# Attention scores head by head in quarters of the TensorE array, and the turned probabilities copied in two parts

## The chip, the cores and the metric

The kernel runs on one core of one Trainium2 chip. The time is that of the whole program on the device in microseconds (us); three runs of the kernel before took 480.45, 480.79 and 478.44 us, median 480.45 us.

TensorE multiplies, VectorE (DVE), ScalarE (ACT) and GpSimd (POOL) work on tiles of 128 partitions, and SyncE (SP) issues most DMAs. In the profile a product on TensorE is two instructions: PEld loads its stationary operand (its weights), PE streams the moving operand through them. A product of fp32 operands shows as two such pairs.

## What is computed

Attention over keys and values averaged in groups of 8, then a mixture of experts on the rows of its output. The shapes: batch 8, heads 8, sequence 576, head size 64, so 4608 tokens of 512 numbers; 8 experts with 1024 hidden units.

```python
k_p = k.reshape(B, H, Sp, pool, D).mean(axis=3)        # Sp = 72 pooled keys
v_p = v.reshape(B, H, Sp, pool, D).mean(axis=3)
scores = scale * np.matmul(q, k_p.transpose(0, 1, 3, 2))
scores = scores - np.max(scores, axis=-1, keepdims=True)
attn = np.exp(scores)
attn = attn / (np.sum(attn, axis=-1, keepdims=True) + 1e-09)
x = np.matmul(attn, v_p)                               # rows of tokens, 512 wide
...
do_compute = x @ w_skip > 0
e_idx = np.argmax(x @ w_gate, axis=1)                  # one expert per token
h = np.maximum(x[mask] @ w1[e], 0.0)
out = x + gate_w * (h @ w2[e])                         # where do_compute
```

## The kernel before

**Stages.** The first stage, attention, takes the 4608 tokens in 36 tiles of 128 queries (in the program t = 0 to 35). A tile belongs to one batch or, for t = 4, 13, 22 and 31, half to one and half to the next. While it runs, the routing of finished tiles to experts is worked out in seven groups (9, 5, 4, 6, 5, 4 and 3 tiles), GpSimd scatters the token numbers of each tile into a table in DRAM (L415), and the weights of one chosen expert are staged and split in high and low parts. The second stage runs the experts, from about 147 us on; first with products for three tiles gathered early (L532 to L552), then in a loop over units of tokens.

**A step of the attention stage.** All engines' orders are fixed when the program is written (a manual schedule; no scheduler moves anything). In step t of the loop at L842 the order is:

1. ScalarE copies the turned probabilities of tile t-2 from PSUM to SBUF, `turned_p` (L328: one instruction, 640 columns); in steps that begin a new batch also the turned sums of values, `turned_v` (L267).
2. VectorE normalises tile t-3 (L355 to L362), whose output rows SyncE stores (L361).
3. TensorE makes the scores of tile t (`scores`, L303). Heads lie two and two on the partitions (head size 64 twice). The 8 heads are 4 pairs; the pooled keys of a pair stand in `kbd` as a block diagonal, so one product of 128 x 128 queries with 144 columns makes both heads of a pair. Pairs 0 and 1 go to one PSUM bank, pairs 2 and 3 to another. A tile on two batches does each product in two halves of 64 queries.
4. VectorE takes minima (L309, one instruction a bank), and ScalarE the exponentials, 8 of 128 x 72 (L315), into `e`.
5. TensorE multiplies the probabilities of tile t-2 with the values (`values`, L341 and L344, 12 pairs of weights and product), then turns the probabilities of tile t-1 (`turn_p`, L323 and L324, five transposes into two PSUM banks `pt`); in some steps it then turns sums of values (`turn_v`, L261 and L262).
6. VectorE, ScalarE and GpSimd do what is due of the side work: sums of keys (L208), key blocks (L213), splitting of weights (L582, L585, L589), steps of the routing (L380 to L465), scatters (L415).

`pt` exists once, the values' bank `o` (L335) once, the probabilities `e` and their copy `pT` twice, the scores' banks three times for two a tile. So the copy of step t waits for the transposes at the end of step t-1, the values wait for the copy and for the normalising of tile t-3, and the transposes come after the values.

**Start and end.** Tiles 0 and 1 are scored before the loop; pair g can be scored as soon as its keys are summed (L208) and laid out (L213). At the end VectorE turns the counts into slots, and when the last scatter has landed GpSimd fetches rows of the table (L1040), TensorE turns them (L1072), and VectorE takes them as slots (L1073 to L1075). On TensorE L1072 stands between the early products in a fixed place; a barrier of all engines follows before the loop over units.

The three lines that fix the places of scores:

```python
sc = ps_s.tile([128, 512], F32, name="sc")[:, 0:4 * SP]          # L300, one bank of half the heads
nc.tensor.matmul(sc[sl, g * 2 * SP:(g + 1) * 2 * SP], qts[t // QG][:, t % QG, half * 2 + g, sl],
                 kbd[b % 2][:, half * 2 + g, :], start=True, stop=True)   # L303
```

Of the kernel before, what the change touches and what calls it, by code (L numbers as in the profile page):

```python
# [26 lines left out]
F32 = mybir.dt.float32  # L27
# [18 lines left out]
VA = HD + 10  # L46
# [117 lines left out]
def attention(tc, nc, q, k, vm, vr, cf, wg, w1, w2, whi, wlo, out, c, pay, offs, table, near, bufs, late, early, mb, fin, cfs):  # L164
    with ExitStack() as ctx:
# [92 lines left out]
        def turn_v(b):  # L258
            tp = pt[:, 1, 128:512].rearrange("p (j n) -> p j n", j=3)
# [39 lines left out]
        def scores(t, half):  # L299
            sc = ps_s.tile([128, 512], F32, name="sc")[:, 0:4 * SP]  # L300
            for g in range(2):
                for sl, b in parts(t):
                    nc.tensor.matmul(sc[sl, g * 2 * SP:(g + 1) * 2 * SP], qts[t // QG][:, t % QG, half * 2 + g, sl],  # L303
                                     kbd[b % 2][:, half * 2 + g, :], start=True, stop=True)
            return sc
# [5 lines left out]
        def exped(e, sc, mn, i):  # L311
            ev = e[:, (4 * SP + GAP) * i:(4 * SP + GAP) * i + 4 * SP].rearrange("p (k g) -> p g k", g=2)
            for h in range(4):
                k0 = (h % 2 ^ i) * SP
                nc.scalar.activation(ev[:, h // 2, k0:k0 + SP], sc[:, h * SP:(h + 1) * SP], AF.Exp,  # L315
                                     bias=mn[:, 4 * i + h:4 * i + h + 1], scale=-1.0)

        def turn_p(e):
            for i in range(2):
                k0 = (4 * SP + GAP + 2 * KL) * i  # L320
                ev = e[:, k0:k0 + 256].rearrange("p (k g) -> p g k", g=2)
                for g in range(2):
                    nc.tensor.transpose(ptf[:, (2 * i + g) * 128:(2 * i + g) * 128 + 128], ev[:, g], ident)  # L323
            nc.tensor.transpose(ptf[:, 512:640], e[:, 256:384], ident)  # L324

        def turned_p():
            pT = ap.tile([128, 5, 128], F32, name="pT")
            nc.scalar.activation(flat(pT), ptf[:, 0:640], AF.Copy)  # L328
            return pT

        def values(t, pT, apart=False):
# [5 lines left out]
            for a, o_ in enumerate(os):  # L337
                ov = o_[:, 0:4 * VA].rearrange("p (g h c) -> p g h c", g=2, h=2)
                for g in range(2):
                    for sl, b in parts(t):  # L340
                        nc.tensor.matmul(o_[sl, g * 2 * VA:(g + 1) * 2 * VA], pT[:, 2 * a + g, sl], vbd[b % 2][:, 2 * a + g, :],  # L341
                                         start=(g == 0), stop=False)
                for sl, b in parts(t):
                    nc.tensor.matmul(ov[sl, :, 1, :], pT[:, 4, sl], vl4[b % 3][:, 2 * a:2 * a + 2, :], start=False, stop=True)  # L344
# [466 lines left out]
        def exponentials(t, sc, mn):  # L811
            es[t] = ebuf[t % 2]
            for i in range(2):
                exped(es[t], sc[i], mn, i)
# [4 lines left out]
        for t in range(2):  # L819
# [3 lines left out]
            sc = [scores(t, i) for i in range(2)]  # L823
# [13 lines left out]
        sc = [scores(2, i) for i in range(2)]  # L837
# [4 lines left out]
        for t in range(2, NT):  # L842
# [11 lines left out]
            if t > 2:  # L854
                normal(t - 3)
                sc = [scores(t, i) for i in range(2)]
# [933 lines left out]
```

## Time and profile before

| what | value |
|---|---|
| median of three runs | 480.45 us (478.44 to 480.79) |
| the profiled execution: time, span | 481.24 us, 479.2 us |
| instructions in the span | 11182 |
| PE busy | 463.5 us (97%), x3043 |
| PEld busy | 417.1 us (87%), x3044 |
| DVE, ACT, POOL busy | 303.4 (63%), 225.7 (47%), 250.3 us (52%) |
| granted TensorE clock, mean | 0.999 |
| HBM read, written | 80.85 MB, 31.21 MB |

The span runs from the first to the last instruction; the profiled execution's own time is 2.0 us longer. Busy is the time in which at least one instruction of an engine was under way. Matmuls are pipelined: a product's duration holds the way through the array, and products of a stream overlap, so that the pace of a stream is read from starts, not from durations. Idle time has a releaser, the instruction that ended the wait as far as the profile shows ("issue": none shown).

### The profile page before, as it was taken

The page shows a single profiled execution, that of the slowest core. Times are in us where ns is not written, and L with a number is a line of the kernel's source. Part 1 is how long each engine was busy: PE and PEld are TensorE (multiplying, and loading weights), DVE is VectorE, ACT ScalarE, POOL GpSimd, SP SyncE. Part 2 cuts the span into 40 slices and gives each one's busy share as a digit, 9 for nine tenths or more (in the row PEclk, how much of TensorE's full clock was granted, in tenths as well). Part 3 has the DMA queues.
Part 4 walks back from the last instruction along what each step waited for, and adds up shares of the span by engine and source line. Part 5 has one row for each costly group of instructions (what it writes and reads, how often), then busy time and mean ns, then how long its engine had stood idle before and what let it go on. Part 6 is the DMA issues. An engine that isn't in the chain of part 4 may idle for free. (4 is left out here: it accounts for less than half of the span.)

```text
span 479.2 us, 11182 instructions
## 1 busy us (share of the span) xinstructions
PE 463.5 (97%) x3043; PEld 417.1 (87%) x3044; DVE 303.4 (63%) x713; ACT 225.7 (47%) x578; POOL 250.3 (52%) x328
## 2 busy tenths in 40 slices
PE   7999999999999999899999999999999999999995
PEld 4799899989999979798989987989899898989894
DVE  5877888798788622578795667663846554343321
ACT  5678768888891211546462645612435251212110
POOL 4499499999998154363342424362624161515242
PEclk9999999999999999999999999999999999999999
DMA  8999999996931026679787497877687223322021
GB/s 278 388 396 390 361 352 332 384 333 207 328 122 68 11 62 215 230 228 308 247 289 244 136 290 241 300 240 251 202 256 262 89 95 101 129 66 88 22 88 42
DMA packets 52042, 103.88 MB, mean 217 GB/s; under 512 B 10031, under 2 KB 22959, under 8 KB 50336
## 3 DMA queue, kind: packets, MB, share of 16 engines
q1 hardware_dynamic: 40544, 78.18, 47.8%
q0 software_dynamic: 11456, 25.22, 15.0%
q8 instruction: 17, 0.28, 0.2%
q14 instruction: 25, 0.20, 0.1%
HBM read 80.85 MB, written 31.21 MB: 234 GB/s over the span
## 5 line engine op out<-in xcount | busy, mean ns | idle before, releaser
L1289 POOL DMA_INDIRECT out<-ring,slot x33 | 35.8, 1085 | 109.3 <-POOLq L1115 105.6
L315 ACT ACTIVATE e<-sc,mn 128x72 f32<-128x72 f32 x288 | 65.0, 345 | 7.4 <-DVE mn L309 6.8
L1527 ACT ACTIVATE hhi<-psl 128x256 fp32r<-128x256 f32 (+3 forms) x59 | 23.5, 400 | 94.0 <-ACTq L1115 93.5
L1384 PE MATMUL psl<-xlo,w1hi 128*128 128x256 f32 (+3 forms) x220 | 64.1, 291 | 0.0
L1383 PE MATMUL psl<-xhi,w1hi 128*128 128x256 f32 (+3 forms) x220 | 64.0, 291 | 0.0
L1385 PE MATMUL psl<-xhi,w1lo 128*128 128x256 f32 (+3 forms) x220 | 64.0, 291 | 0.0
L1284 POOL DMA_INDIRECT ring<-out,slot x42 | 46.6, 1109 | 22.6 <-issue 22.4
L341 PE MATMUL o<-vbd,pT 128*128 128x148 f32 (+1 forms) x312 | 49.4, 298 | 1.1 <-DVE x L360 1.1
L1626 DVE SCALAR_TENSOR_TENSOR hlo<-psl,hhi 128x256 fp32r<-128x256 f32 (+2 forms) x55 | 23.2, 423 | 41.3 <-DVEq L1115 39.0
L415 POOL DMA_INDIRECT table<-pay,r_di x36 | 36.7, 1018 | 12.6 <-DVE mb L443 6.4
L1383 PEld LDWEIGHTS psl<-xhi,w1hi 128*128 128x128 f32 x220 | 41.3, 188 | 0.8 <-issue 0.4
L1384 PEld LDWEIGHTS psl<-xlo,w1hi 128*128 128x128 f32 x220 | 41.3, 188 | 0.5
L341 PEld LDWEIGHTS o<-vbd,pT 128*128 128x128 f32 (+1 forms) x312 | 38.6, 179 | 3.6 <-ACT ring L213 1.0
L1385 PEld LDWEIGHTS psl<-xhi,w1lo 128*128 128x128 f32 x220 | 41.2, 187 | 0.0
L1297 POOL DMA_DIRECT2D sorted<-ring x39 | 22.2, 572 | 32.9 <-DMA ring<-out,slot 25.8
L1603 DVE TENSOR_TENSOR w2lo<-stage,w2hi 128x1024 fp32r<-128x1024 f32 x28 | 34.3, 1223 | 6.6 <-DVEq L1115 6.4
L1384 PE MATMUL psd<-xlo,w1hi 128*128 128x256 f32 (+3 forms) x132 | 38.4, 291 | 0.0
L1385 PE MATMUL psd<-xhi,w1lo 128*128 128x256 f32 (+3 forms) x132 | 38.4, 291 | 0.0
L1383 PE MATMUL psd<-xhi,w1hi 128*128 128x256 f32 (+3 forms) x132 | 38.4, 291 | 0.0
L1409 PE MATMUL mb<-w2hi,hlo 128*128 128x512 f32 x88 | 34.8, 396 | 0.0
L1409 PE MATMUL psf<-w2hi,hlo 128*128 128x512 f32 x88 | 34.8, 396 | 0.0
L1407 PE MATMUL psf<-w2hi,hhi 128*128 128x512 f32 x88 | 34.8, 395 | 0.0
(276 smaller groups left out, 1216.0 us busy)
## 6 DMA issues: line engine op xcount, KB each, us to landing
stage<-in_w SPq DMA_DIRECT2D x64, 512.0 KB, 5.5
sorted<-ring POOLq DMA_DIRECT2D x39, 256.0 KB, 3.3
out<-x SPq DMA_DIRECT2D x36, 256.0 KB, 5.4
stage<-in_k SPq DMA_DIRECT2D x6, 1152.0 KB, 8.8
blocks<-sorted SPq DMA_DIRECT2D x100, 64.0 KB
qt<-in_q SPq DMA_DIRECT2D x9, 512.0 KB, 7.4
hhi<-in_vm SPq DMA_DIRECT2D x4, 1024.0 KB, 7.7
hlo<-in_vm SPq DMA_DIRECT2D x3, 1024.0 KB, 9.8
```

Of the source, the lines that this page charges most:

```text
L315: nc.scalar.activation(ev[:, h // 2, k0:k0 + SP], sc[:, h * SP:(h + 1) * SP], AF.Exp, bias=mn[:, 4 * i + h:4 * i + h + 1], scale=-1.0)
L341: nc.tensor.matmul(o_[sl, g * 2 * VA:(g + 1) * 2 * VA], pT[:, 2 * a + g, sl], vbd[b % 2][:, 2 * a + g, :], start=(g == 0), stop=False)
L415: m = nc.gpsimd.indirect_dma_start(table, bass.IndirectOffsetOnAxis(ap=di[:, j:j + 1], axis=0), flat(fin["pays"][:, t0 + j:t0 + j + TW // ...
L1284: g.indirect_dma_start(ring[:, (s + 3) % 9, 0:D], None, out, bass.IndirectOffsetOnAxis(ap=slot[:, s:s + 1], axis=0), bounds_check=NTOK - 1 ...
L1289: g.indirect_dma_start(out, bass.IndirectOffsetOnAxis(ap=offsets, axis=0), ring[:, (s + 3) % 9, 0:D], None, bounds_check=NTOK - 1, oob_is_ ...
L1383: t.matmul(ps, whi[0][:, k, w], xhi[:, k, xs], start=(k == 0), stop=False)
L1384: t.matmul(ps, whi[0][:, k, w], xlo[:, k, xs], start=False, stop=False)
L1385: last = t.matmul(ps, wlo[0][:, k, w], xhi[:, k, xs], start=False, stop=(k == 3))
L1407: t.matmul(ps, hhi[:, k, sl], whi[1][:, k, :], start=(k == 0), stop=False)
L1409: last = t.matmul(ps, hlo[:, k, sl], whi[1][:, k, :], start=False, stop=(k == 7))
L1527: a.activation(hhi[:, f, xs], bank(f, xs, alone), AF.Relu).then_inc(sem["act"], 1)
L1603: v.tensor_tensor(chunk_of(wlo, c), chunk_view(stage[c], c), chunk_of(whi, c).bitcast(F32), ALU.subtract).then_inc(sem["wlo1" if c < 4 els ...
```

## The change

The scores of a tile are made head by head. A head lies on one half of the partitions, so each product takes 64 partitions of queries, 64 queries and the 72 columns of its own keys: 16 products a tile instead of 4 (or 8 in a tile on two batches), each in one quarter of the array (half of its rows, half of its columns). The order is pair by pair; within a pair first the lower 64 queries, then the upper; within these first the head on the lower partitions, then the one on the upper. Heads on the lower partitions go to one PSUM bank, those on the upper to the other; the exponentials follow this order, to the same places of `e`. `kbd` keeps its layout; its zeros are not read any more. The copy of the turned probabilities becomes two instructions of 384 and 256 columns, one from each bank of `pt`, to two tiles; the transposes go three to the first bank and two to the second, and `turn_v` uses other columns of the two banks.

```diff
         def turn_v(b):
-            tp = pt[:, 1, 128:512].rearrange("p (j n) -> p j n", j=3)
+            tp = ptf[:, 384:768].rearrange("p (j n) -> p j n", j=3)
             for j in range(2):
                 nc.tensor.transpose(tp[:, j, :], vss[b][:, j * 128:j * 128 + 128], ident)
             nc.tensor.transpose(tp[:, 2, :], lss[b], ident)
@@ -296,36 +296,41 @@
             b0, b1 = t * 128 // S, (t * 128 + 127) // S
             return [(slice(0, 128), b0)] if b0 == b1 else [(slice(0, 64), b0), (slice(64, 128), b1)]
 
-        def scores(t, half):
-            sc = ps_s.tile([128, 512], F32, name="sc")[:, 0:4 * SP]
-            for g in range(2):
-                for sl, b in parts(t):
-                    nc.tensor.matmul(sc[sl, g * 2 * SP:(g + 1) * 2 * SP], qts[t // QG][:, t % QG, half * 2 + g, sl],
-                                     kbd[b % 2][:, half * 2 + g, :], start=True, stop=True)
+        def scores(t):
+            sc = [ps_s.tile([128, 512], F32, name="sc")[:, 0:4 * SP] for _ in range(2)]
+            for g in range(4):
+                for i, sl in enumerate(halves):
+                    b = (t * 128 + i * 64) // S
+                    for r, o in zip(halves, range(2)):
+                        nc.tensor.matmul(sc[o][sl, g * SP:(g + 1) * SP], qts[t // QG][r, t % QG, g, sl],
+                                         kbd[b % 2][r, g, o * SP:(o + 1) * SP], start=True, stop=True)
             return sc
 
         def least(sc, mn, i):
 
             nc.vector.tensor_reduce(mn[:, i * 4:i * 4 + 4], sc.rearrange("p (h k) -> p h k", k=SP), axis=AX.X, op=ALU.min)
 
-        def exped(e, sc, mn, i):
-            ev = e[:, (4 * SP + GAP) * i:(4 * SP + GAP) * i + 4 * SP].rearrange("p (k g) -> p g k", g=2)
-            for h in range(4):
-                k0 = (h % 2 ^ i) * SP
-                nc.scalar.activation(ev[:, h // 2, k0:k0 + SP], sc[:, h * SP:(h + 1) * SP], AF.Exp,
-                                     bias=mn[:, 4 * i + h:4 * i + h + 1], scale=-1.0)
+        def exped(e, sc, mn, o):
+            for g in range(4):
+                i = g // 2
+                ev = e[:, (4 * SP + GAP) * i:(4 * SP + GAP) * i + 4 * SP].rearrange("p (k g) -> p g k", g=2)
+                k0 = (o ^ i) * SP
+                nc.scalar.activation(ev[:, g % 2, k0:k0 + SP], sc[:, g * SP:(g + 1) * SP], AF.Exp,
+                                     bias=mn[:, 4 * o + g:4 * o + g + 1], scale=-1.0)
 
         def turn_p(e):
             for i in range(2):
                 k0 = (4 * SP + GAP + 2 * KL) * i
                 ev = e[:, k0:k0 + 256].rearrange("p (k g) -> p g k", g=2)
                 for g in range(2):
-                    nc.tensor.transpose(ptf[:, (2 * i + g) * 128:(2 * i + g) * 128 + 128], ev[:, g], ident)
-            nc.tensor.transpose(ptf[:, 512:640], e[:, 256:384], ident)
+                    nc.tensor.transpose(pt[:, i, (2 * i + g) * 128:(2 * i + g) * 128 + 128], ev[:, g], ident)
+                if i == 0:
+                    nc.tensor.transpose(pt[:, 0, 256:384], e[:, 256:384], ident)
 
         def turned_p():
-            pT = ap.tile([128, 5, 128], F32, name="pT")
-            nc.scalar.activation(flat(pT), ptf[:, 0:640], AF.Copy)
+            pT = [ap.tile([128, 3 - i, 128], F32, name=f"pT{i}") for i in range(2)]
+            for i, sl in enumerate((slice(0, 384), slice(256, 512))):
+                nc.scalar.activation(flat(pT[i]), pt[:, i, sl], AF.Copy)
             return pT
 
         def values(t, pT, apart=False):
@@ -338,10 +343,10 @@
                 ov = o_[:, 0:4 * VA].rearrange("p (g h c) -> p g h c", g=2, h=2)
                 for g in range(2):
                     for sl, b in parts(t):
-                        nc.tensor.matmul(o_[sl, g * 2 * VA:(g + 1) * 2 * VA], pT[:, 2 * a + g, sl], vbd[b % 2][:, 2 * a + g, :],
+                        nc.tensor.matmul(o_[sl, g * 2 * VA:(g + 1) * 2 * VA], pT[a][:, g, sl], vbd[b % 2][:, 2 * a + g, :],
                                          start=(g == 0), stop=False)
                 for sl, b in parts(t):
-                    nc.tensor.matmul(ov[sl, :, 1, :], pT[:, 4, sl], vl4[b % 3][:, 2 * a:2 * a + 2, :], start=False, stop=True)
+                    nc.tensor.matmul(ov[sl, :, 1, :], pT[0][:, 2, sl], vl4[b % 3][:, 2 * a:2 * a + 2, :], start=False, stop=True)
             return [o_.unsqueeze(1) for o_ in os] if apart else [o]
 
         def normalised(t, os):
@@ -810,8 +815,8 @@
 
         def exponentials(t, sc, mn):
             es[t] = ebuf[t % 2]
-            for i in range(2):
-                exped(es[t], sc[i], mn, i)
+            for o in range(2):
+                exped(es[t], sc[o], mn, o)
@@ -820,7 +825,7 @@
...
-            sc = [scores(t, i) for i in range(2)]
+            sc = scores(t)
             exponentials(t, sc, softmax(t, sc))
...
```

On TensorE, in a step in which a tile's queries are of one batch (names: `sc` scores, `pT` the copied probabilities, `pt` the PSUM they are turned in), the rows before, from the scores to the transposes:

```order
L303 MATMUL sc<-ring,qt 128x144 [waits DMAHW3_49]
L303 MATMUL sc<-ring,qt 128x144
L303 MATMUL sc<-ring,qt 128x144 [waits DVE_49,Activation_49]
L303 MATMUL sc<-ring,qt 128x144
L341 MATMUL o<-vbd_121,pT 128x148 [waits DVE_49,Activation_49]
L341 MATMUL o<-vbd_121,pT 128x148
L344 MATMUL o<-vl_123,pT 128x2x74
L341 MATMUL o<-vbd_121,pT 128x148 x2
L344 MATMUL o<-vl_123,pT 128x2x74
L323 MATMUL pt<-cfs,e_127 128x128 x4
L324 MATMUL pt<-cfs,e_127 128x128
```

and the same step now:

```order
L305 MATMUL sc<-ring,qt 64x72 [waits DMAHW3_49]
L305 MATMUL sc<-ring,qt 64x72 [waits DVE_49,Activation_49]
L305 MATMUL sc<-ring,qt 64x72 x14
L346 MATMUL o<-vbd_121,pT_685 128x148 [waits DVE_49,Activation_49]
L346 MATMUL o<-vbd_121,pT_685 128x148
L349 MATMUL o<-vl_123,pT_685 128x2x74
L346 MATMUL o<-vbd_121,pT_686 128x148 [waits Activation_49]
L346 MATMUL o<-vbd_121,pT_686 128x148
L349 MATMUL o<-vl_123,pT_685 128x2x74
L326 MATMUL pt<-cfs,e_127 128x128 x2
```

Four products became sixteen in the same place; the wait for ScalarE's exponentials of the tile before moved from the third product to the second, and the second half of the values has a wait of its own for the second copy.

At the start of the program on TensorE, from the first scores to the first transposes of tile 1, before:

```order
L303 MATMUL sc<-ring,qt 128x144 [waits DMAHW1_49,Activation_49,Pool_49]
L303 MATMUL sc<-ring,qt 128x144 [waits Activation_49] x3
L303 MATMUL sc<-ring,qt 128x144 [waits DMAHW5_49]
L303 MATMUL sc<-ring,qt 128x144
L303 MATMUL sc<-ring,qt 128x144 [waits DVE_49,Activation_49]
L303 MATMUL sc<-ring,qt 128x144
L817 MATMUL o<-ring 128x512
```

and now:

```order
L305 MATMUL sc<-ring,qt 64x72 x2
L305 MATMUL sc<-ring,qt 64x72 [waits Activation_49] x2
L305 MATMUL sc<-ring,qt 64x72 x2
L305 MATMUL sc<-ring,qt 64x72 [waits DMAHW5_49]
L305 MATMUL sc<-ring,qt 64x72 [waits DVE_49,Activation_49]
L305 MATMUL sc<-ring,qt 64x72 x14
L822 MATMUL o<-ring 128x512
```

Both banks of tile 0 are now complete only after the keys of the last pair, and all of tile 1 but its first product stands behind the wait for exponentials of tile 0.

## Rows read from the trace of the kernel before

**Rows 1.** Windows by stage: PE, PEld, DVE, ACT, POOL busy (x instructions), PEclk, DMA share, GB/s.
```profile
50.00:75.00 25.00, 24.39 (x214) 22.89 (x214) 22.18 (x81) 19.16 (x69) 17.91 (x19) 1.00 0.97 356
```

**Rows 2.** Timeline of one step, all engines: start us, us, what [idle before <-releaser].
```profile
85.55 0.27 PE L324 MATMUL pt<-cfs,e 128*128 128x128 f32 x1
...
85.66 1.15 PE L303 MATMUL sc<-ring,xhi 128*128 128x144 f32 x8
...
85.92 0.71 ACT L328 ACTIVATE pT<-pt 128x640 f32<-128x640 f32 x1 [0.30 <-PE pt L324]
...
86.68 0.55 PEld L341 LDWEIGHTS o<-vbd,pT 128*128 128x128 f32 x4
...
88.76 0.27 PE L324 MATMUL pt<-cfs,e 128*128 128x128 f32 x1
...
88.89 0.68 DVE L360 TENSOR_TENSOR x<-o,rc 128x512 f32<-128x512 f32 x1
```

**Rows 3.** Timeline of PE and PEld about tiles on two batches, four stretches.
```profile
122.86 0.27 PE L262 MATMUL pt<-cfs,ls 128*128 128x128 f32 x1
123.06 1.20 PE L303 MATMUL sc<-ring,xlo 128*64 128x144 f32 x16
...
123.06 0.14 PEld L303 LDWEIGHTS sc<-ring,xlo 128*64 128x64 f32 x2 [0.17 <-issue]
...
33.81 0.29 PE L344 MATMUL o<-ring,pT 128*64 128x148 f32 x1
...
34.03 0.32 PEld L323 LDWEIGHTS pt<-cfs,e 128*128 128x128 f32 x2 [0.20 <-issue]
```

**Rows 4.** Timeline of PE: short products of the routing.
```profile
91.60 0.26 PE L399 MATMUL mb<-r_oh,ones 128*128 128x40 bf16 x4
...
91.71 0.18 PE L401 MATMUL mb<-r_oh,upper 128*128 128x32 bf16 x1
```

**Rows 5.** Timeline of POOL, first and last scatter; windows of POOL between.
```profile
55.78 1.08 POOL L415 DMA_INDIRECT table<-pay,r_di  x1 [6.39 <-DVE mb L443]
...
58.35 0.99 POOL L415 DMA_INDIRECT table<-pay,r_di  x1 [0.17 <-issue]
...
155.03 0.98 POOL L415 DMA_INDIRECT table<-pay,r_di  x1 [0.30 <-issue]
...
125.00:152.40 27.40, 24.77 (x30) 1.00 0.47 167
```

**Rows 6.** The source line L1072: duration ns min/median/max, first and last start us.
```profile
L1072 PEld LDWEIGHTS o<-cfs,stage x2: 189/190/191, 162.6 to 162.8; 81*128 81x128 f32 x2
...
L1072 PEldq EVENT_SEMAPHORE  x1: 1459/1459/1459, 160.7 to 160.7; - x1
```

**Rows 7.** Timeline of the start: ACT, DVE, PE.
```profile
8.78 0.54 ACT L213 ACTIVATE ring<-kp 64x72 f32<-64x72 f32 x2 [0.25 <-DVE kp L208]
9.34 3.73 ACT L315 ACTIVATE e<-sc,mn 128x72 f32<-128x72 f32 x16
...
8.66 0.45 DVE L309 TENSOR_REDUCE mn<-sc 128x4 f32<-128x288 f32 x1
...
13.71 0.75 PE L323 MATMUL pt<-cfs,e 128*128 128x128 f32 x4 [0.30 <-ACT pT L328]
```

**Rows 8.** Timeline of DVE, the normalising that opens step 11.
```profile
48.56 0.21 DVE L355 RECIPROCAL rc<-o 128x8 f32<-128x8 f32 x1 [0.53 <-PE o L344]
```

**Rows 9.** Timeline of ACT: a copy of 384 columns.
```profile
27.89 0.48 ACT L267 ACTIVATE vT<-pt 128x384 f32<-128x384 f32 x1
```

**Rows 10.** Windows after the last product; then groups of PE by shape, mean ns last.
```profile
474.30:477.90 3.60, 0.00 (x0) 0.00 (x0) 0.75 (x1) 0.00 (x0) 0.97 (x1) 1.00 0.03 10
478.20:479.10 0.90, 0.00 (x0) 0.00 (x0) 0.00 (x0) 0.00 (x0) 0.00 (x0) 0.50 0.20 75
...
L739 PE MATMUL o<-ring 128*128 128x512 f32 x6 | 5.5, 1084 | 1.7 <-POOL ring L717 1.7
...
L817 PE MATMUL o<-ring 128*128 128x512 f32 x6 | 3.1, 593 | 0.0
```

More of the change, by code (lines that the diff above doesn't have):

```diff
@@ L836, in attention @@
         gates_dve(0)
-        sc = [scores(2, i) for i in range(2)]
+        sc = scores(2)
         mn = softmax(2, sc)
@@ L855, in attention @@
                 normal(t - 3)
-                sc = [scores(t, i) for i in range(2)]
+                sc = scores(t)
             if t == NT - 1:
```

## The prediction

> **What bounds the kernel now.** I read a window of the attention stage first. From 50 to 75 us TensorE is busy for 24.39 of 25 us, DVE for 22.18 and ACT for 19.16 [rows 1]. The change touches only the attention stage, so the questions are what ends a step there, and whether a shorter stage makes the rest start earlier.
>
> The timeline of one step answers the first. I measure from T, the start of the last transpose (85.55). ACT starts the copy of the probabilities at T+0.37, it takes 0.71, and the weights of the values are loaded at 86.68, T+1.13. In between TensorE does the scores, from 85.66 on: 8 products in 1.15, their last start 0.29 before the end, so 0.123 each, and the stream is over at T+1.09. The next T is 88.76, 2.08 after the values' load; the step lasts 3.21 [rows 2]. So scores and copy run side by side and end within 0.04 us of each other: shorter scores help only as far as the copy gets shorter too. A third loop is as tight: the normalising of the step's x ends at 88.89 + 0.68 = 89.57, 2.89 after the values' load [rows 2], and the next values must wait for it.
>
> The second answer is GpSimd. It waits 6.39 us for the routing of the first nine tiles, starts the first scatter at 55.78 and the last at 155.03. In between it is never free: the idle times before scatters are 0.17 or 0.30 with no releaser, and from 125 to 152.4 it is busy for 24.77 of 27.4 us with that 0.17 between its instructions [rows 5]. The last scatter leads to the fetched table rows, for which TensorE's queue waited at L1072 from 160.7 for 1.459 us, until 162.16; the weights there were loaded at 162.6 [rows 6]. So TensorE comes to that place only some 0.5 us after the data. **Whatever TensorE gains beyond 0.5 us, it waits off at L1072, unless GpSimd's chain starts earlier at 55.78.**
>
> **The change part by part.**
>
> *Switch to quarters.* A plain step has no switch of the array's shape now; the tiles on two batches have. There the first load of half-width weights comes 0.20 after the start of the last full transpose (122.86 to 123.06), where a load inside a stream is ahead of its product [rows 3]. Back, the next full load comes 0.22 after the start of the last half-width product (33.81 to 34.03); 0.126 of this is its 148 columns, so 0.09 remains [rows 3]. The trace shows no quarter; I take these two for it, since they are the nearest, also half a shape.
>
> *Sixteen products for four.* With half the columns each (72 for 144) a pair of instructions streams for 0.061 instead of 0.123 [rows 2]. Whether quarters run side by side is not shown, but halves are: 16 pairs of 144 columns took 1.20, where 8 full ones took 1.15 [rows 2, 3]. So each half did its own 8 in the full pace. Four quarters side by side: first load 0.05 (what 1.20 has over 7 paces and the last 0.29), 7 paces of 0.061, and some 0.02 of offset: 0.50. Lower bound of the stretch: this. Upper bound: all 32 pairs one after another, 1.95. A middle: what feeds them, since four short products began between 91.60 and 91.71, one each 0.027 [rows 4], 0.86 for 32. I take 0.50, nearest to the rows on halves, which are also fp32 products with their own weights.
>
> The scores then end, and a load may follow, at T + 0.20 + 0.50 + 0.06 + 0.09 = T+0.85, before it was T+1.09.
>
> *Two copies for one.* 384 columns take 0.48 [rows 9], 640 take 0.71 [rows 2], so 256 take some 0.37, together 0.14 more; consecutive copies overlap by about 0.1, which leaves 0.05 on ACT. The second copy has no wait for TensorE in the changed order, so the first waits for all five transposes: it starts at T+0.37 as now and ends at T+0.85; the values follow at T+0.90. The second copy ends some 0.3 later, and its half of the values comes 0.75 later: hidden. **A plain step saves 0.23, of which I take 0.20**, because ACT now gets its minima after both banks and its 8 exponentials end later against T, and because the x of the step is ready at 2.89 + 0.05 after the values' load where TensorE could be there after 2.08 + 0.90 = 2.98, so that any other DVE work eats the rest. In steps that begin a batch the copy of the value sums follows the two copies, and TensorE waits for that; I count 0.05 lost.
>
> *Exponentials, minima, values, place of the turned sums:* same number, same size, same queue; nothing, hidden or not. No DMA is added or moved.
>
> *The start.* Before, half of tile 0's heads are ready with the second pair of keys: the minimum is taken at 8.66 and the exponentials start at 9.34, right after the last keys (8.78 + 0.54) [rows 7]. Now both banks need the last keys: products and their way through the array 0.4, the minimum 0.45, so the exponentials start at about 10.25, 0.9 late. Behind the second product of tile 1 all of its scores wait for tile 0's first four exponentials (to 11.2), are done at 12.0, and the exponentials of tile 1 start at 12.5 instead of going on without a break: they end at 14.3 instead of 13.07. Transposes of tile 1 waited for the first copy until 13.71 [rows 7]; they come at 14.7, 1.0 late. TensorE's next scores give back 0.3: **0.65 lost at the start**, with 0 (if keys of later steps come from DMA no earlier anyway) and 1.2 as bounds.
>
> *Until the first scatter.* The nine tiles' routing hangs on step 11's normalising (48.56) [rows 8]. Steps 4 to 10 come before: five plain ones save 1.0, two that begin a batch lose 0.1. With the start: 1.0 - 0.1 - 0.65 = 0.25 us earlier.
>
> *The sum.* GpSimd's chain, and with it the data for L1072, comes 0.25 earlier; TensorE's own 0.5 of delay there goes. Gain 0.75 us; the profiled execution would take 481.24 - 0.75 = 480.5. It lies 0.8 above the median of the runs, so I predict 480.45 - 0.75 = **479.7 us**. TensorE saves some 3 us more in steps 11 to 35 (about 20 plain ones, some held by DVE), and waits them off at L1072, some 2.5 us.
>
> **The rivals.**
>
> *GpSimd does not hold it.* If its chain gets shorter by as much as the steps, the 3.25 us all count: 477.2. For it: TensorE is the busiest engine [rows 1]. Against it: no idle time between its scatters but the fixed one [rows 5]. Chance 0.15.
>
> *The quarters are fed too slowly* (0.86 for the 32 pairs): scores end at T+1.2, no step saves, the start's loss stays: 481.2. The half-width loads speak against it: two begun within 0.14, each of them that long [rows 3]. Chance 0.08.
>
> *Weight loads on the same rows queue up.* Loads of 64 columns come 16 in 0.93 + 0.14 [rows 3], which alone would also fit loads one behind another at 0.053. If so, the 16 loads of each row half take 0.85, scores end at T+1.25, 27 plain steps lose 0.11 each and the start 0.65: 484.1. The Trainium skill has this as a rule (TensorE: Matmul & The Clock Gate, Part 3: Packing small matmuls): a weight load overlaps a running product only where the row group differs. The two loads at 123.06 use the same rows and other columns, and they overlap [rows 3], so the trace disagrees. Chance 0.05.
>
> *Row halves do not run side by side.* No row shows two products on different rows. Then 16 pairs follow each other in each column half, 0.98 for 0.50 - 0.02: T+1.40 instead of T+1.13, and 27 plain steps lose 0.28 each, the start 0.65 and its own scores 0.3: 489 us. It decides as soon as the 16 products take over 0.75 a tile. Chance 0.11. All four quarters in turn, which would mean the change does not do what it says: 1.95, 1.3 lost in each of 33 steps: 523. Chance 0.03.
>
> *The clock falls at L1072.* With no product after 474.3 the granted clock was still 1.00 until 477.9 and 0.50 (1.2 GHz of 2.4) at 478.2 [rows 10]. A wait of over 3.6 us at L1072 could do the same; the first products of the program took 1.084 at that level against 0.593 [rows 10], so some 5 us after it would take 2.5 longer: 482.2. My wait is 2.5. Chance 0.08.
>
> **How the numbers follow.** The forecast has 0.50; its own range is 477.8 to 481 (the start between 0 and 1.2, the step between 0.1 and 0.23). The range 476 to 484 leaves out half of the first rival below and the row halves and the turn by turn above. A difference under 0.5% (2.4 us) can't be told from none here. Faster by more: the first rival and a fifth of the forecast, 0.25. Slower by more: queued loads, row halves, all in turn and a part of the clock, 0.21. Within: 0.54.
>
> **What would show it.** Right: in a plain step 16 products in some 0.75 from first start to last end; the values' load at T+0.9; steps of about 3.0; first exponentials at 10.25; the first scatter near 55.5 and the last near 154.8; TensorE waiting some 2.5 us before L1072. Wrong: a first scatter or a GpSimd chain that moves by over 1 us, scores that still fill 1.1 us, or a copy that ends later than T+1.1.

## The result: slower, by 5 us

The changed kernel took 486.04 us (median of 20 runs, 480.75 to 489.60), the kernel before 480.89 (20 runs, 478.44 to 484.91). The ratio is 1.0075, 95% interval 1.0047 to 1.0103; it leaves out runs more than 1.5% above the fastest, so it lies below the ratio of the medians, 1.0107. The forecast was 479.7 with a range of 476 to 484: the wrong side. The profiled execution took 486.88 us, its span is 484.8 (before 479.2), its mean granted clock 0.989 (0.999).

The plain steps did what was forecast. Timeline of one step of the changed kernel, PE, PEld and ACT, columns as in [rows 2]:

```profile
87.17 0.40 PE L326 MATMUL pt<-cfs,e 128*128 128x128 f32 x2
...
87.50 0.73 PE L305 MATMUL sc<-ring,xhi 64*64 64x72 f32 x32
87.67 0.77 ACT L333 ACTIVATE pT<-pt 128x384 f32<-128x384 f32 x2
...
88.22 0.55 PEld L346 LDWEIGHTS o<-vbd,pT 128*128 128x128 f32 x4
...
90.17 0.40 PE L326 MATMUL pt<-cfs,e 128*128 128x128 f32 x2
```

The last transpose starts 0.11 into the first row, so T = 87.28 (T is the start of the last transpose, as in the prediction). The 16 products fill 0.73 us instead of 1.15, the values' weights are loaded at T+0.94 instead of T+1.13, and the step lasts 3.00 instead of 3.21 [rows 2]. The scores of a step take 0.4 us less and the step became only 0.2 shorter, so in the window of [rows 1] TensorE is now busy for less of the time and waits for more of it:

```profile
50.00:75.00 25.00, 22.88 (x380) 20.88 (x379) 22.24 (x81) 19.77 (x78) 16.62 (x18) 1.00 0.90 318
```

The time went at the start and in steps 26 and 29. Against the kernel before, TensorE is 3.5 us late at the scores of tile 2, 2.3 at tile 12, 1.3 at tile 26, 3.8 at tile 27 and 5.25 at tile 35.

**The start.** Timelines of ACT and PE, windows of PE (us, busy, PEclk, DMA share, GB/s), and last a row of PE before:

```profile
9.03 0.55 ACT L213 ACTIVATE ring<-kp 64x72 f32<-64x72 f32 x2 [0.73 <-DVE kp L208]
10.51 1.80 ACT L318 ACTIVATE e<-sc,mn 128x72 f32<-128x72 f32 x8 [0.94 <-DVE mn L311]
13.28 1.80 ACT L318 ACTIVATE e<-sc,mn 128x72 f32<-128x72 f32 x8 [0.97 <-DVE mn L311]
```

```profile
9.34 0.64 PE L305 MATMUL sc<-ring,qt 64*64 64x72 f32 x10 [0.64 <-ACT ring L213]
11.52 1.23 PE L305 MATMUL sc<-ring,qt 64*64 64x72 f32 x30 [1.54 <-ACT e L318]
12.68 2.07 PE L822 MATMUL o<-ring 128*128 128x512 f32 x2
...
17.15 0.39 PE L326 MATMUL pt<-cfs,e 128*128 128x128 f32 x2
...
20.66 0.73 PE L305 MATMUL sc<-ring,qt 64*64 64x72 f32 x32
```

```profile
7.00:10.00 3.00, 2.18 (x35) 1.00 1.04 346
10.00:12.00 2.00, 0.48 (x16) 0.54 1.09 326
12.00:16.00 4.00, 4.00 (x34) 0.50 1.00 388
```

```profile
17.18 1.23 PE L303 MATMUL sc<-ring,qt 128*128 128x144 f32 x8
```

TensorE waits 1.54 us for the exponentials of tile 0, and in that wait the clock falls to 0.50 (1.2 GHz of 2.4); it stays there until 17.0. The scores of tile 2 begin at 20.66, before at 17.18. Counted from the end of the last keys (L213; 9.58 here, 9.32 before [rows 7]) that is 11.08 us instead of 7.86, 3.2 more.

**Steps 26 and 29.** The first expert's weights come in pieces, and a piece is split in a high part and a low part (piece minus high part). GpSimd makes most low parts, VectorE the second half of pieces 2 and 3 (`w1lo`). Timelines of DVE, POOL and PE, windows of PE, and last step 26 of PE before:

```profile
104.31 2.79 DVE L594 TENSOR_TENSOR w1lo<-stage,w1hi 128x512 fp32r<-128x512 f32 x1
```

```profile
104.68 0.64 POOL L254 TENSOR_TENSOR ring<-ls,cfs 96x256 f32<-96x256 f32 x1
105.25 1.29 POOL L590 TENSOR_TENSOR w1lo<-stage,w1hi 128x512 fp32r<-128x512 f32 x1
```

```profile
105.04 0.73 PE L305 MATMUL sc<-ring,qt 64*64 64x72 f32 x32
108.23 0.74 PE L346 MATMUL o<-vbd,pT 128*128 128x148 f32 x4 [2.45 <-DVE x L365]
...
112.29 0.83 PE L305 MATMUL sc<-ring,qt 64*64 64x72 f32 x32
...
122.86 0.74 PE L346 MATMUL o<-vbd,pT 128*128 128x148 f32 x4 [1.72 <-DVE x L365]
```

```profile
105.70:109.10 3.40, 0.95 (x13) 1.00 0.88 323
109.10:112.60 3.50, 3.50 (x27) 0.51 0.56 188
```

```profile
103.75 1.15 PE L303 MATMUL sc<-ring,qt 128*128 128x144 f32 x8
...
108.49 1.25 PE L303 MATMUL sc<-ring,qt 128*128 128x144 f32 x8
```

In step 26 VectorE makes a low part in 2.79 us, beside two operations of GpSimd; x is normalised late, TensorE waits 2.45 us for it, and from 109.1 on, 0.9 after that wait, the clock is at 0.50 for 3.4 us. The step lasts 7.25 us instead of 4.74. In step 29 the second low part takes 2.67 us, and TensorE waits 1.72 us for x; the clock stays at 1.00, and the step lasts 4.71 us instead of 3.23. The same line in both kernels (before, then changed; ns min/median/max):

```profile
L589 DVE TENSOR_TENSOR w1lo<-stage,w1hi x2: 1162/1502/1841, 102.8 to 114.7; 128x512 fp32r<-128x512 f32 x2
```

```profile
L594 DVE TENSOR_TENSOR w2lo<-stage,w2hi x5: 681/683/684, 126.7 to 166.6; 128x512 fp32r<-128x512 f32 x5
...
L594 DVE TENSOR_TENSOR w1lo<-stage,w1hi x2: 2669/2730/2790, 104.3 to 118.9; 128x512 fp32r<-128x512 f32 x2
```

These losses reach the end. Timeline of POOL, first and last scatter and the waits of over 0.8 us between, answering [rows 5]; then the source line that was L1072 [rows 6]:

```profile
58.31 1.08 POOL L420 DMA_INDIRECT table<-pay,r_di  x1 [6.51 <-DVE mb L448]
...
136.14 0.98 POOL L420 DMA_INDIRECT table<-pay,r_di  x1 [0.81 <-DVE offs L433]
138.33 1.81 POOL L590 TENSOR_TENSOR w2lo<-stage,w2hi 128x512 fp32r<-128x512 f32 x1 [1.21 <-ACT w2hi L587]
...
151.16 0.98 POOL L420 DMA_INDIRECT table<-pay,r_di  x1 [0.87 <-DVE offs L433]
...
160.09 0.98 POOL L420 DMA_INDIRECT table<-pay,r_di  x1 [0.30 <-issue]
```

```profile
L1077 PEld LDWEIGHTS o<-cfs,stage x2: 189/190/191, 168.2 to 168.4; 81*128 81x128 f32 x2
...
L1077 PEldq EVENT_SEMAPHORE  x1: 1379/1379/1379, 166.2 to 166.2; - x1
```

The first scatter is 2.53 us later than before, the last one 5.06, so the chain between them takes 101.78 us instead of 99.25: GpSimd, never free before, now waits for engines that run late. The weights at the fetched rows are loaded 5.6 us later, and the rest of the program is as long as before: all of the 5.6 us of span.

### The profile page after: what moved, and what is told of

It is laid out like the page before. It is cut to its first block, busy times and chain, and to the rows that moved or that the text cites. A ratio compares the mean times of both kernels' runs of the same rounds, so it can differ in the third digit from the quotient of the medians.

```text
span 484.8 us, 12888 instructions
## 1 busy us (share of the span) xinstructions
PE 458.8 (95%) x3875; PEld 407.4 (84%) x3876; DVE 305.2 (63%) x713; ACT 227.7 (47%) x614; POOL 250.5 (52%) x328
## 5 line engine op out<-in xcount | busy, mean ns | idle before, releaser
L311 DVE TENSOR_REDUCE mn<-sc 128x4 f32<-128x288 f32 x72 | 29.6, 452 | 10.3 <-PE sc L305 7.9
L333 ACT ACTIVATE pT<-pt 128x384 f32<-128x384 f32 x72 | 27.6, 436 | 16.3 <-PE pt L326 12.8
```

What stands on the lines that cost most here:

```text
L311: nc.vector.tensor_reduce(mn[:, i * 4:i * 4 + 4], sc.rearrange("p (h k) -> p h k", k=SP), axis=AX.X, op=ALU.min)
L333: nc.scalar.activation(flat(pT[i]), pt[:, i, sl], AF.Copy)
```

## The experiments

**Theory A:** two waits of TensorE, at the start and at step 26, each with a fall of the clock, make up the loss; the steps themselves are 0.2 us shorter. (Theory A as it was put on record leaves out the wait in step 29; the zeros of the experiments take out both subtractions.) **Rival R:** products in quarters cost by themselves, wherever they stand. Median, and ratio to the kernel before beside it on the same chip:

| kernel | us | ratio, 95% |
|---|---|---|
| e1 start by pairs | 480.38 | 1.0024 [0.9997, 1.0050] |
| e2 start filled | 482.92 | 1.0068 [1.0045, 1.0091] |
| e3 zeros for low parts | 480.46 | 1.0005 [0.9988, 1.0022] |
| e4 both (e1, e3) | 478.08 | 0.9953 [0.9933, 0.9972] |
| e5 before, two copies | 480.70 | 1.0000 [0.9983, 1.0016] |
| e6 changed, one copy | 483.31 | 1.0069 [1.0037, 1.0101] |
| e7 before, zeros | 479.38 | 0.9967 [0.9944, 0.9989] |
| e8 low parts shared anew | 481.39 | 1.0018 [0.9995, 1.0040] |
| e9 changed | 488.24 | 1.0168 [1.0145, 1.0191] |
| e10 filled, zeros | 484.49 | 1.0063 [1.0022, 1.0105] |
| e11 quarter-filled, zeros | 487.35 | 1.0148 [1.0107, 1.0190] |
| e12 low parts earlier | 481.65 | 1.0027 [0.9998, 1.0056] |
| e13 changed | 484.33 | 1.0089 [1.0054, 1.0123] |
| e14 start by pairs | 481.15 | 1.0030 [1.0005, 1.0054] |
| e15 zeros | 479.74 | 0.9994 [0.9975, 1.0013] |
| e16 both | 477.92 | 0.9961 [0.9942, 0.9980] |
| e17 low parts later | 483.55 | 1.0074 [1.0047, 1.0102] |
| e18 second one later | 480.60 | 1.0001 [0.9977, 1.0024] |

e1 to e4, e5 to e8, e9 to e12, e13 to e16, and e17 with e18 each ran on one chip.

### The four corners

The start's edit (`scores_by_pair` and `exped_by_pair` are the functions of before) and the zeros:

```diff
-            sc = scores(t)
+            sc = [scores_by_pair(t, i) for i in range(2)]
...
-                exped(es[t], sc[o], mn, o)
+                (exped if t > 1 else exped_by_pair)(es[t], sc[o], mn, o)
```

```diff
         def low_v(cc, i):
+            if cc in (2, 3):
+                nc.vector.memset(piece(wlo, cc, i).bitcast(F32), 0.0)
+                return
```

Start by pairs, first run and again beside the other corners:

> The changed kernel, but tiles 0 and 1 scored by pairs and exponentiated by halves as before. Theory A (two waits of TensorE, one at the start, one at tile 26, each followed by a fall of the granted clock; the steps themselves are 0.2 us shorter; GpSimd's chain of scatters sets the end): the scores of tile 2 begin at 17.2 us (changed kernel 20.66), no fall of the clock in the first 100 us, first scatter at 54.6 (58.31). The wait before the values of tile 24 stays, since TensorE and GpSimd both move earlier by about the same: over 1.5 us, with a fall of the clock behind it. Time 481.5 to 483.5. Rival R (products in quarters let the clock fall by themselves, wherever they are): the clock falls at other places of the first 100 us too and the time stays within 1 us of the changed kernel's 486.

> The changed kernel with tiles 0 and 1 by pairs. Theory A: 2.5 to 5 us under the changed kernel; 0 to 1.5 over the kernel before, since the wait behind the low part stays. If the quarters as such cost more than the start: within 1.5 of the changed kernel.

Zeros:

> The changed kernel, but the two low parts of the first weights that VectorE makes beside GpSimd's adds (pieces 2 and 3) are filled with zeros and not subtracted. Leaves out those two parts of the split. Theory A: VectorE is not held by GpSimd, no wait over 1 us before the values of tiles 24 to 28 and no second fall of the clock; scores of tile 35 at 139 us instead of 143.9; no scatter after 127 us waits for another engine, the last one is at 157.5 (2.5 after that of the kernel before, as the first); time 483.4. Rival R: the clock falls there anyway; time 485 to 486. Second rival (the filling takes as long on VectorE beside GpSimd as the subtraction, 1.8 us or more): no change.

> The changed kernel with zeros for the low parts of pieces 2 and 3 (left out). Theory A: 3 to 5 us under the changed kernel; as the kernel before, within 1.5.

Both:

> Both edits: tiles 0 and 1 as before, and the two low parts filled with zeros (left out). Theory A: first scatter at 54.6, last at 153.9, no fall of the clock before the fetch of table rows; time 479.7, 1.2 under the kernel before, TensorE waiting 3 us or more for the table rows (if the clock falls there, up to 2.5 more). Rival R: 484 or more.

> Both edits. Theory A: 1.5 to 2.5 us under the kernel before and 0 to 1.5 under the kernel before with zeros alone (1.2 under it); nothing is left for the quarters as such. If the quarters as such cost: over the kernel before with zeros, by as much as they cost.

The changed kernel beside them, and once on another chip:

> The changed kernel, beside the next three on one chip. Theory A: 4 to 6 us over the kernel before.

> The changed kernel as it is, once more on the chip of the next three. Theory A: a fall of the clock at the start; VectorE's first low part over 2.5 us, with TensorE waiting over 2 us at tile 26; ratio to the kernel before between 1.005 and 1.011. If the first result was an accident of where the waits fell: under 1.003.

The zeros in the kernel before:

> The kernel before with VectorE's low parts of pieces 2 and 3 filled with zeros (left out): what this edit is worth without the change. If GpSimd's chain sets the end: the chain from first to last scatter is 1.5 us shorter than 99.25 (as in the changed kernel with this edit, 97.75) and the time 1.5 us lower, 478.7. If TensorE's steps set it: the same chain, TensorE waits longer for the table rows, and the time stays at 480.1.

On the chip of e13 to e16, in per cent over the kernel before: changed 0.89, start by pairs 0.30, zeros -0.06, both -0.39. So the start costs 0.59 with the low parts and 0.33 without, 2.8 and 1.6 us; the low parts cost 0.95 and 0.69, 4.6 and 3.3 us. In the kernel before the same zeros bring 0.33 (e7, on another chip). What is left of the change without either is -0.39 + 0.33 = -0.06%, and by e4 -0.47 + 0.33 = -0.14%: 0.3 and 0.7 us gained, with some 1.4 of uncertainty either way. R would have had a loss there. So on the chips of e1 to e4 and e13 to e16 R falls, and the start and the two subtractions make up the loss. The four times of e13 to e16 came out as expected; e4 came out 1.6 us under its 479.7.

e1 came out at 480.38 where 481.5 to 483.5 was expected, but the wait that was to stay did (in its profile the clock did not fall behind it; in e14 the low part began beside a scatter, took 0.68, and there was no wait). The row of e1:

```profile
105.07 0.74 PE L361 MATMUL o<-vbd,pT 128*128 128x148 f32 x4 [2.47 <-DVE x L380]
```

e3 was expected at 483.4 and came out 3 us lower: its last scatter is at 154.98, not 157.5. Its first scatter is 1.1 us earlier than in the changed kernel (57.23; the clock was at 0.50 for 3.4 us, not 6.8), and its chain takes 97.75 us where 99.25 was taken. GpSimd, too, is held by VectorE's subtraction: before, a sum of 96 x 64 and a scatter beside the two subtractions took 0.78 and 1.27 us, with zeros (e7) 0.31 and 1.01.

e9 lost more than any other, 1.0168, where 1.005 to 1.011 was expected, and it did not show what was expected at step 26. In its profile the clock fell at the start, but VectorE's two low parts took 0.69 and 0.68 us, the first beside a scatter, and there was no long wait for x behind them. (That profile is of its fastest run, 483.56 us; the other five took 487.1 to 488.4.) So the loss in step 26 is no fixed price of the change: it depends on what GpSimd does when the subtraction comes. For that chip see below.

### What the start costs, and why

e2 fills TensorE's two waits with products of constants, 256 columns ahead of the last pair of tile 0, 512 and 256 behind it:

```diff
+                if between and g == 3:
+                    between()
...
+            if t == 0:
+                constant_product()
+                half_product()
```

> The changed kernel with products of constants (256, 512 and 256 columns) in the two waits of TensorE at the start, before the last pair of tile 0 and before tile 1; nobody reads them. Theory A: the clock stays at 1.00 through the start; what is lost there by the order alone stays: scores of tile 2 at 18.9 us (20.66 in the changed kernel, 17.18 before), first scatter 56.5; the wait at tile 24 stays; time 484.3. Rival R: the clock falls although TensorE has work, scores of tile 2 stay near 20.7, time 486.

Windows of PE in e2:

```profile
7.00:10.00 3.00, 1.72 (x18) 1.00 1.06 348
10.00:12.00 2.00, 2.00 (x14) 1.00 1.08 304
12.00:16.00 4.00, 3.45 (x43) 1.00 0.97 360
```

The clock stays. From the last keys to the scores of tile 2 it takes 9.33 us: of the 3.2 us lost there, 1.5 are the order's and 1.75 the clock's. The clock's share is not fixed: in the other profiles of this start without fillers (e3, e6, e9, e13, e15) the same stretch took 10.1 to 11.3 us, with the clock at 0.50 for 3.4 or 6.8 us. The wait at step 26 is there as expected, 2.47 us with a fall of the clock, and the time is 482.92, 1.4 under what was expected.

e10 and e11 take the low parts away and fill with products of the whole array, or of one quarter (`init[0:64, 0:64]` as weights, 64 partitions moving):

> The changed kernel with the two waits at the start filled with products of constants, full width, and with zeros for the low parts of pieces 2 and 3 (left out), so that only the start is seen. Theory A: clock 1.00 at the start, scores of tile 2 9.3 us after the last keys (11.1 in the changed kernel, 7.9 before); mean clock of the runs 0.996 to 1.0 as with the start by pairs (0.990 to 0.996 without filling); time 0.8 to 1.2 us under the one without filling (480.46), 479.4.

> The same with filling products of as many columns that stand in one quarter of the array (64 partitions, 64 results). TensorE is busy as long. If the clock goes by whether TensorE works: all as with full-width filling, 479.4. If products on a quarter hold it up less: the clock falls at the start, mean clock of the runs 0.990 to 0.996, time 480.5 as without filling.

Windows of PE, e10, then e11:

```profile
7.00:10.00 3.00, 2.65 (x36) 1.00 1.04 350
10.00:12.00 2.00, 2.00 (x36) 1.00 1.06 362
12.00:16.00 4.00, 3.44 (x29) 1.00 1.03 399
```

```profile
7.00:10.00 3.00, 2.19 (x27) 1.00 1.04 343
10.00:12.00 2.00, 1.75 (x25) 0.91 1.12 363
12.00:16.00 4.00, 4.00 (x35) 0.62 1.01 391
```

With quarters the clock fell at about 11.6, with whole products it did not fall at the start. Quarter fillers run beside the scores, so TensorE was a little less busy than in e10; against e2, where the clock held, it was busier from 7 to 10 and less busy from 10 to 12. With one profile each this does not settle whether products in quarters bear on the clock. The mean clocks of the runs, 0.992 to 0.998 (e10) and 0.981 to 0.998 (e11), do not settle it either, since in both profiles the clock fell again later: to 0.50 at 92.2 in e10 and at 93.6 in e11, for 6.8 us each. In e12, with the start by pairs, it fell at 92.7.

Both times are 5 and 7 us over what was expected, and that is a loss that Theory A has no place for. In all four profiles of that chip (e9 to e12) VectorE is idle for 1.2 us before its minima of tiles 18 and 21 and for 2.4 before those of tile 22, and these begin 0.7, 1.4 and 1.2 us after the scores' recorded end. Behind the late minima come late exponentials and late key blocks, for which TensorE waits. Row of PE in e10:

```profile
90.79 0.71 PE L307 MATMUL sc<-ring,xlo 64*64 64x72 f32 x26 [0.97 <-ACT ring L213]
```

Of the other profiles only those of e6 (tile 22) and e8 (tiles 18 and 32) show minima over 0.9 us late. What delays them stays open, since no releaser in the trace accounts for the delay. The kernel before took 480.26 us on that chip, about as on the others, but there is no profile of it from there. So for that chip it is not shown that the start and the low parts make up the loss, and R is not ruled out there. e10's profile is of its slowest run, 487.94 us.

### Each half of the change alone

e5 is the kernel before with the two copies and their five transposes, e6 the changed kernel with the one copy of 640 columns.

> The kernel before with the two copies alone (scores by pairs as before, five transposes in two banks, 384 and 256 columns copied). Prediction's account (scores end at T+1.09 and copy at T+1.07, each holds the values almost alike): a plain step goes from 3.21 to 3.17 at most, the scores of tile 12 begin 0.2 to 0.4 us earlier, no loss at the start, no fall of the clock; time as before within 0.7 us. Rival (the copies carry the whole gain of the steps): plain steps of 3.0.

> The changed kernel with one copy of 640 columns as before (scores in quarters). Prediction's account: plain steps of 3.2, since the copy holds the values; the loss at the start as in the changed kernel (scores of tile 2 begin 3.2 us later after the last keys than before, with a fall of the clock). TensorE then keeps its place against GpSimd as in the kernel before, so VectorE's low part at tile 26 takes under 2 us and the clock does not fall there; time 3 us over the kernel before, 483. Rival: plain steps of 3.0 also without the second copy, and the long low part as in the changed kernel, 486.

Timelines of PE, two steps each, e5, then e6:

```profile
79.39 1.15 PE L303 MATMUL sc<-ring,qt 128*128 128x144 f32 x8
80.38 0.67 PE L343 MATMUL o<-vbd,pT 128*128 128x148 f32 x4
...
82.46 1.15 PE L303 MATMUL sc<-ring,xhi 128*128 128x144 f32 x8
```

```profile
80.99 0.73 PE L305 MATMUL sc<-ring,qt 64*64 64x72 f32 x32
81.91 0.77 PE L344 MATMUL o<-vbd,pT 128*128 128x148 f32 x4 [0.19 <-ACT pT L331]
...
84.19 0.73 PE L305 MATMUL sc<-ring,xhi 64*64 64x72 f32 x32
```

Copies alone give steps of 3.07, quarters alone 3.20, both 3.01. Quarters alone free TensorE early only to wait for the copy, as expected; the copies alone brought 0.14, over three times the 0.04 that the account allowed; of it 0.03 to 0.07 lie between scores and values (0.99 for 1.02 to 1.06), the rest behind the values. In e5 that gain, too, shifted VectorE: its first low part took 2.55 us, TensorE waited 1.69 for x, and the time is that of before. e6 carries the start's loss (10.1 us from the last keys to the scores of tile 2), its first low part, in step 25, takes 0.68, and it loses 3 us, as expected.

### Where the low part stands

All four have the start by pairs. e8 gives GpSimd both parts of pieces 2 and 3 and VectorE those of 4 and 5:

```diff
-            if cc > 1 and i:
+            if cc > 3 and (i or cc < 6):
```

e12 moves VectorE's parts of 2 and 3 ahead of the sum of keys of their step:

```diff
+                if cc < 4:
+                    dve.items.insert(0, (now["t"] + 1, -1, now["t"] + 1, 0.65, lambda: low_v(cc, i)))
+                    return
```

e17 moves them to later steps (e18 the same with `{2: 0, 3: 2}`):

```diff
-                dve.add(now["t"] + 1, now["t"] + 2, 0.65, lambda: low_v(cc, i))
+                d = {2: 1, 3: 2}.get(cc, 0)
+                dve.add(now["t"] + 1 + d, now["t"] + 2 + d, 0.65, lambda: low_v(cc, i))
```

> The changed kernel with tiles 0 and 1 by pairs and with the low parts shared out in another way, nothing left out: GpSimd makes both low parts of pieces 2 and 3, VectorE both of pieces 4 and 5, when GpSimd only fills and scatters. Theory A: no low part on VectorE over 0.8 us, no wait of TensorE over 1 us before values, no fall of the clock; GpSimd has as much work as before but is not held; time 477.5 to 479, as with both edits and zeros (478.1). Rival (GpSimd's added work before 125 us delays scatters that later fills can't make up): 480 or more.

> The changed kernel with tiles 0 and 1 by pairs, and with VectorE's low parts of pieces 2 and 3 one instruction earlier, ahead of the sum of keys of their step (0.7 us); nothing is left out. Theory A (what decides is whether one of GpSimd's adds of two operands is under way): the first one falls beside GpSimd's scatter and takes 0.68 instead of 2.8, TensorE waits under 1 us at tile 26; the second one lies in a row of adds and still takes 1 to 2.5. Time 479.2 to 480, about 0.5 to 1 under the one with the low parts in their old place (480.38). Rival (VectorE is held wherever it stands in the step): no difference.

> Tiles 0 and 1 by pairs; VectorE's low part of piece 2 one step later, of piece 3 two steps later; nothing left out. Theory A (the place against GpSimd's rows of adds decides): the second one stands beside fetches and fills and takes 0.68; the first one under 1.5; time 478.5 to 480, ratio to the kernel before 0.997 to 1.0. If the loads that wait for the room of these pieces (at tiles 26 and 30) become late and hold SyncE's queue: 481 or more.

> The same, with only the second one (piece 3) two steps later. Theory A: the first one keeps its chance (0.68 to 2.8 with the run), the second takes 0.68: 479.5 to 480.5, between the corner with the start by pairs (480.4 to 481.2) and the one above.

None of them gave a kernel that is faster than the kernel before. e8 (481.39, expected 477.5 to 479): VectorE's other low parts were held as well (1.58 and 2.26 us), and GpSimd's chain is 99.87 us; the rival held. e12 (481.65, expected 479.2 to 480): the first part began beside a subtraction of GpSimd, not a scatter, and took 1.64; TensorE waited 1.94 for x. It ran on the chip of e9, so the late minima are in its time as well. e17 (483.55, expected 478.5 to 480) and e18 do not do what their expectations say: the later place stands behind the load into the same room, so the subtraction waits for the next piece and takes its numbers (that part of the split is changed). In e17 VectorE waited 4.64 us for the load and TensorE 4.67:

```profile
108.97 0.69 DVE L609 TENSOR_TENSOR w1lo<-stage,w1hi 128x512 fp32r<-128x512 f32 x1 [4.64 <-DMA stage<-in_w]
```

In e18 the first part took 2.81 and TensorE waited 2.47, the second, beside GpSimd's fetches, took 0.69: the time, 480.6, is that of the corner with the start by pairs, as expected (479.5 to 480.5) but for 0.1.

## Why the prediction was wrong, step by step

Two steps of the sum failed. It has the first scatter 0.25 us earlier, with 0.65 lost at the start: the start lost 3.2, and the first scatter came 2.53 later. And it takes GpSimd's chain behind that scatter as fixed: it grew by 2.53, to 101.78 us, with waits of GpSimd behind steps 26 and 29, in which TensorE lost 4.0 us. Together the last scatter is 5.06 late. Both are signs of being wrong that the prediction itself names.

*Steps, quarters, copies:* right in size. The stretch of 0.75 measured 0.73, T+0.90 measured T+0.94, 3.0 measured 3.0. With that the rivals of slow feeding, queued weight loads (the 32 loads of a tile fill 0.58 us), row halves in turn and all in turn fall. The sharing out was wrong: the account had scores and copy end together, so that neither part would do much alone, but the copies alone bring 0.14 of the 0.20.

*The start* **is the first step that failed:** its mechanism was right, its size not, and the clock was left out. Exponentials at 10.25 were forecast and came at 10.51, with keys 0.26 later. Where the clock holds (e2) those of tile 1 end 1.25 later against the keys than before, as forecast; in the changed kernel they end 1.8 later. But the sum carried only 1.0 of that to the transposes and took back 0.3 by the next scores, which no row bears out: 3.47 us from the transposes of tile 1 to those scores before, 3.62 in e2. The 0.65 measures 1.5. And the clock was not thought of here at all: another 1.75. It was looked for only at L1072, behind a wait longer than the 3.6 us of [rows 10], though the change puts a wait of TensorE into a start with waits on both sides; the clock fell here in a wait of 1.54.

*That GpSimd's chain, never free, fixes the end* was right of the kernel before: with zeros its chain is 98.29 us instead of 99.25 and starts 0.3 earlier, and the time falls by 1.2 (e7). It also holds where TensorE runs ahead: with both edits TensorE waited 3.31 us for the fetched rows (e16):

```profile
L1095 PEldq EVENT_SEMAPHORE  x1: 3308/3308/3308, 157.6 to 157.6; - x1
```

It was wrong as a rule for the changed kernel, where GpSimd waited for engines that had fallen behind: 101.78 us.

*"TensorE saves some 3 us more in steps 11 to 35"* **is the second step that failed.** From the scores of tile 12 to those of tile 26 it saved 1.0 (50.60 us for 51.59); then step 26 took back 2.5 and step 29 another 1.5, and TensorE lost 3.0 from tile 12 to tile 35. The prediction said that other work of DVE eats the rest, but priced that work as it stood. Saving 0.2 a step, and losing time at the start, move VectorE against GpSimd, whose chain keeps its own pace, and where they meet changes. The rows to see it were in the trace of before: two subtractions of 1.16 and 1.84 us where five others of the same shape take 0.68. Where they meet after a change is partly chance: the first of the two took 2.79 and 2.82 us in two profiles of the changed kernel and 0.69 in the third (e9).

*The clock at L1072:* TensorE waited 1.38 there, 3.31 in e16, and the clock fell behind neither. *The end:* from the scatters on the program is as long as before, as forecast.

## What to carry to other kernels

Where one engine's chain sets the end and the others run beside it, a shorter step shifts them against it: look for one instruction whose durations spread far beyond its usual one, and ask what it meets when it comes a microsecond earlier. Leave the first tiles out of a change that makes an operand complete later, since there nothing stands behind it, and a wait of TensorE may cost the clock as well. And try the parts alone: here the cheap one, two copies, had most of the step's gain and none of the loss at the start, and still gained nothing at the end.

## What the runs showed of the hardware

*VectorE and GpSimd hold each other.* In the 20 profiles VectorE's subtraction of two operands in SBUF (128 x 512) took 0.67 to 0.74 us 63 times (the last two of each profile, which stand in one row, are left out). The 23 others took 1.00 to 2.82, and each of them ended 0.55 to 0.56 us after the end of an operation of GpSimd with two operands, the last of an unbroken row of them. Beside GpSimd's fills, fetches and scatters alone it was not held. GpSimd is held as well: the low part beside VectorE's took 1.81 at 138.33, 1.28 alone. The Trainium skill (SBUF — State Buffer, Who interferes with whom) has the two sharing a pair of ports when VectorE has two operands in SBUF and GpSimd reads SBUF, the one that issues first blocking the other. The trace agrees that one is held to the other's end; it does not show that the first to begin wins: at 104.31 VectorE's record begins 0.37 before GpSimd's, and it ends last.

*The clock fell about short waits of TensorE, and not at the same point of them.* In the changed kernel it fell at 10.15, in a wait of 1.54 us, and at 109.1, 0.9 after a wait of 2.45; in e13 at 9.16, in a wait of 0.40 and ahead of one of 1.54; in e10 at 92.2, behind waits of 0.97 and 0.55. In e1 it did not fall behind a wait of 2.47. It is not tied to quarters: in e18, with the start by pairs and late keys, it was 0.50 from 10 to 12, too.

*Quarters run side by side.* 16 products (32 instructions) take 0.73 us, where 8 of half width and 144 columns (16 instructions) took 1.20 [rows 3]; after the last transpose the first starts at T+0.22, against T+0.11 for whole products [rows 2], so the switch into quarters costs 0.1; the prediction had T+0.20.
